# Loading one activation block behind the V weights instead of ahead of them, at the start of a fused attention and gated-MLP kernel

## The chip, the cores and the metric

The kernel runs on one core of one Trainium2 chip. The metric is the device time of one execution in microseconds (us). A ratio given with an interval is computed as the mean time of one kernel's runs over that of the other kernel's runs of the same rounds, so it is not quite the ratio of the medians that are quoted beside it. A profile is one execution taken by the hardware profiler; its times count from the start of the span. A transfer's landing is the last of the 16 increments of its semaphore (a counter that others wait on) in the trace; these (5.84 to 6.47 us for the V weights of the kernel before) are taken as one from each of the 16 DMA engines that the page names. The granted clock is the share of PE's full clock that the trace records for a stretch.

Engines: PE is TensorE (matmuls), PEld its weight loads (for a transpose of a block they load `xn`, for a V matmul the transposed block `xnT`; the V weights are the other operand), DVE is VectorE, ACT is ScalarE, POOL is GpSimd, SP is the sync engine, which issues 54 of the 56 DMAs in the trace of the kernel before.

## The reference, cut to what matters

```python
x = A_x                                  # 1 x 2048 x 512, bf16
xn = _layernorm(x, axis=-1)              # (x - mean) / sqrt(var + 1e-5), row by row
return x + _A_ref(xn, A_wqkv, A_wo) + _B_ref(xn, B_w_gate, B_w_up, B_w_down)
# _A_ref: 32 heads of 16, causal attention in a window of 256; qkv = xn @ wqkv, then @ wo
# _B_ref: ((xn @ w_gate) * (xn @ w_up)) @ w_down, inner size 1792
```

## The kernel before

The 2048 rows are 16 blocks of 128 rows, four blocks to a chunk. Before PE can do useful work, the blocks of the first chunk must be loaded, normalised, transposed and multiplied with the V weights. These are the loads (`self.x[:, t, :]` is block t; the first 512 columns of `Wqkv` are Q, then K, then V):

```python
for lo, hi in ((0, 1), (1, 2), (2, 4)):
    nc.sync.dma_start(out=self.x[:, lo:hi, :], in_=xv[:, lo:hi, :])
for lo in (1024, 512, 0):                      # V, K, Q weights, 512 KB each
    nc.sync.dma_start(out=self.Wqkv[:, :, lo:lo + 512], in_=wq[:, :, lo:lo + 512])
# ... gate, up, x blocks 4 to 7, gate, up, down, Wo: cut ...
for lo, hi in ((8, 10), (10, 12), (12, NT)):
    nc.sync.dma_start(out=self.x[:, lo:hi, :], in_=xv[:, lo:hi, :])
```

And this is the order of work on the first chunk. `norm_stats` is two DVE instructions (statistics `st`, then mean and variance `mv`), `norm_scale` computes the inverse deviation `rs` on POOL (for block 0 partly on DVE), `norm_apply` makes the normalised block `xn` on DVE, `norm_transpose` is four PE transposes with a copy by ACT, `proj_v` four V matmuls with a copy to `V`.

```python
def first_chunk(self):
    self.new_chunk(0)
    for b in range(2):
        self.norm_stats(b, 1)
        self.norm_scale(b, 1)
    for b in (0, 1, 2):
        self.norm_apply(b)
        if b < 2:
            self.norm_stats(b + 2, 1)
            self.norm_scale(b + 2, 1)
    self.norm_transpose(0, False)
    self.keep_busy(8)                          # spare matmuls
    for b in range(4):
        if b < 3:
            self.norm_transpose(b + 1, False)
        self.proj_v(b, engine="act" if b == 2 else "dve")
        if b == 0:
            self.norm_apply(3)
    # ... K and Q projections, copies of V by DMA from ACT's queue: cut ...
```

The softmax here doesn't subtract the row's maximum and nothing guards it: scores larger than these inputs give would overflow.

## Time and profile before

| what | value | where from |
|---|---|---|
| time | 263.29 us, median of 3 (263.16 to 263.78) | timed runs |
| profiled span | 261.2 us, PE busy 98% | head and first part of the page |
| first V matmul | 6.67 us | timeline of PE |
| first K matmul | 10.76 us | timeline of PE |
| V weights landed | 6.47 us | semaphore increments in the trace |

A span with PE busy for 98% is read as one long line of matmuls: whatever delays PE by a microsecond at the start should be there at the end too, unless PE later waits for something that does not move with it. The lines behind this are shown in the prediction.

### The profile page before, as it was taken

How to read it: one execution, taken by the hardware profiler on the slowest of the kernel's cores; microseconds unless marked ns; L12 is line 12 of the kernel's file. 1: busy time of each engine (PE TensorE's matmuls, PEld its weight loads, DVE VectorE, ACT ScalarE, POOL GpSimd, SP SyncE). 2: the span in 40 equal slices, each digit the busy share in tenths (PEclk: the TensorE clock that was granted, in tenths of full speed). 3: DMA queues.
4: the chain of work that ended last, by engine and by line, in shares of the span. 5: the costliest groups of instructions: out<-in, count | busy, mean ns of one | idle time of the engine just before them, and what ended most of it. 6: DMA issues, size and time to landing. Idle time of an engine off the chain costs nothing.

```text
span 261.2 us, 7718 instructions
## 1 busy us (share of the span) xinstructions
PE 255.8 (98%) x3154; PEld 118.0 (45%) x3170; DVE 179.5 (69%) x357; ACT 176.4 (68%) x143; POOL 116.0 (44%) x278
## 2 busy tenths in 40 slices
PE   8999999999999999999999999999999999999995
PEld 8444444444344544444544454344544445444453
DVE  6787888779846597557974769767795235977344
ACT  3477688888757776678775567767787546787600
POOL 6225342425457644333457644544443451464600
PEclk9999999999999999999999999999999999999999
DMA  6999910120012300002001310001000100000002
GB/s 193 379 350 341 286 30 20 24 48 1 3 37 46 83 3 1 3 0 48 3 3 40 84 43 3 0 1 29 23 3 0 42 24 20 5 0 3 1 3 83
DMA packets 19427, 15.05 MB, mean 58 GB/s; under 512 B 7360, under 2 KB 19392, under 8 KB 19392
## 3 DMA queue, kind: packets, MB, share of 16 engines
q1 hardware_dynamic: 18848, 14.26, 18.6%
q8 instruction: 26, 0.43, 0.7%
q10 hardware_dynamic: 544, 0.30, 0.4%
q14 instruction: 9, 0.07, 0.1%
HBM read 9.70 MB, written 2.10 MB: 45 GB/s over the span
## 4 chain that ended last, share of the span: by engine, by line
PE 98%; issue 1%; DVE 0%
PE gp L399 19%; PE up L410 19%; PE psd L432 17%; PE qkp L255 11%; PE S L317 10%; PE acc L370 7%; PE vp L243 5%; PE psd L438 5%; PE L L432 2%; PE wps L131 2%; PE L L438 1%; PE xTp L213 0%; PE L L370 0%; DVE x L448 0%; DVE idle L95 0%
## 5 line engine op out<-in xcount | busy, mean ns | idle before, releaser
L323 ACT ACTIVATE P<-S 128x2048 bf16<-128x2048 f32 x75 | 140.7, 1876 | 49.6 <-PE S L317 41.0
L162 POOL TENSOR_SCALAR_AFFINE_SELECT P<-P 64x256 bf16<-64x256 bf16 x224 | 99.7, 445 | 123.7 <-ACT P L323 108.6
L399 PE MATMUL gp<-xnT,Wg 128*128 128x512 bf16 x224 | 60.1, 380 | 0.0
L410 PE MATMUL up<-xnT,Wu 128*128 128x512 bf16 x224 | 59.1, 380 | 0.0
L415 DVE TENSOR_TENSOR hT<-up,gsb 128x512 bf16<-128x512 f32 x56 | 38.3, 684 | 18.3 <-PE up L410 13.1
L432 PE MATMUL psd<-Wd,hT 128*128 128x512 bf16 (+1 forms) x202 | 46.9, 369 | 0.8 <-issue 0.6
L347 DVE TENSOR_TENSOR P<-P,diag 128x512 bf16<-128x512 bf16 (+1 forms) x75 | 29.6, 394 | 5.9 <-ACT P L323 5.9
L432 PEld LDWEIGHTS <-hT 128*128 128x128 bf16 x238 | 21.3, 98 | 25.3 <-issue 3.5
L410 PEld LDWEIGHTS <-Wu 128*128 128x128 bf16 x224 | 20.4, 98 | 25.6 <-issue 3.3
L399 PEld LDWEIGHTS <-Wg 128*128 128x128 bf16 x224 | 20.3, 98 | 25.3 <-issue 3.3
L317 PE MATMUL S<-Q,K 32*128 32x320 bf16 (+4 forms) x720 | 29.8, 254 | 0.1
L255 PE MATMUL qkp<-xnT,Wqkv 128*128 128x512 bf16 x128 | 29.9, 380 | 0.0
L234 ACT ACTIVATE gsb<-gp 128x512 bf16<-128x512 f32 x38 | 22.3, 596 | 7.7 <-PE gp L399 6.9
L317 PEld LDWEIGHTS <-K 32*128 32x128 bf16 x720 | 10.3, 92 | 30.7 <-issue 30.3
L376 DVE STREAM_TRANSPOSE at<-acc 128x512 f32<-128x512 f32 x30 | 19.1, 688 | 6.5 <-PE acc L370 6.4
L448 DVE TENSOR_TENSOR x<-psd,x 128x512 bf16<-128x512 f32 (+1 forms) x15 | 9.7, 655 | 15.7 <-PE psd L438 15.7
L255 PEld LDWEIGHTS <-Wqkv 128*128 128x128 bf16 x128 | 11.7, 98 | 14.7 <-issue 1.8
L370 PE MATMUL acc<-P,VS 64*32 64x320 bf16 (+4 forms) x672 | 17.7, 253 | 0.0
L370 PE MATMUL acc<-P,V 64*32 64x320 bf16 (+4 forms) x672 | 17.5, 253 | 0.0
L370 PEld LDWEIGHTS <-V 64*32 64x32 bf16 x720 | 15.1, 91 | 2.3 <-issue 1.7
L243 PE MATMUL vp<-Wqkv,xnT 128*128 128x512 bf16 x60 | 14.9, 380 | 0.3 <-issue 0.2
L370 PEld LDWEIGHTS <-VS 64*32 64x32 bf16 x720 | 14.7, 91 | 0.6 <-issue 0.2
(54 smaller groups left out, 180.5 us busy)
## 6 DMA issues: line engine op xcount, KB each, us to landing
out_dram<-x SPq DMA_DIRECT2D x15, 128.0 KB, 1.8
Wg<-in_B_w_gate_dram SPq DMA_DIRECT2D x2, 896.0 KB, 11.2
Wu<-in_B_w_up_dram SPq DMA_DIRECT2D x2, 896.0 KB, 12.6
Wd<-in_B_w_down_dram SPq DMA_DIRECT2D x1, 1792.0 KB, 17.4
Wqkv<-in_A_wqkv_dram SPq DMA_DIRECT2D x3, 512.0 KB, 6.3
x<-in_A_x_dram SPq DMA_DIRECT2D x2, 512.0 KB, 8.6
VS<-V SPq DMA_DIRECT2D x6, 144.0 KB, 2.6
x<-in_A_x_dram SPq DMA_DIRECT2D x3, 256.0 KB, 4.8
```

The costliest lines, as they stand in the source:

```text
L162: nc.gpsimd.affine_select(out=v, in_=v, pattern=pattern + [[1 if diag else -1, 64]], compare_op=ALU.is_ge if diag else ALU.is_gt, fill=0.0 ...
L234: nc.scalar.activation(out=out, in_=in_, func=ACT.Copy)
L243: nc.tensor.matmul(ps[:], lhsT=self.xnT[T][:, b, k, :], rhs=self.Wqkv[:, k, 1024:1536], start=(k == 0), stop=(k == 3))
L255: nc.tensor.matmul(ps[:], lhsT=self.Wqkv[:, k, lo:lo + 128], rhs=self.xnT[T][:, :, k, :], start=(k == 0), stop=(k == 3))
L317: nc.tensor.matmul(S[:, e, col:col + n], lhsT=self.K[U, c][rows, keys], rhs=self.Q[T, c][rows, q:q + n], start=True, stop=True, tile_posit ...
L323: nc.scalar.activation(out=P[:, :, 0:col], in_=S[:, :, 0:col], func=ACT.Exp, scale=0.25)
L347: self.nc.vector.tensor_tensor(out=v, in0=v, op=ALU.min, in1=self.diag.unsqueeze(1).unsqueeze(1).to_broadcast([128, 4, n, 64]))
L370: nc.tensor.matmul(accs[par][32 * e:32 * e + 32, q:q + n], lhsT=v, rhs=P[rows, e, col:col + n], start=(i == 0), stop=(i == len(todo) - 1), ...
L399: nc.tensor.matmul(ps[:], lhsT=self.Wg[:, k, 128 * f:128 * f + 128], rhs=self.xnT[T][:, :, k, :], start=(k == 0), stop=(k == 3))
L410: nc.tensor.matmul(ps[:], lhsT=self.Wu[:, k, 128 * f:128 * f + 128], rhs=self.xnT[T][:, :, k, :], start=(k == 0), stop=(k == 3))
L415: nc.vector.tensor_tensor(out=self.hT[T, f][:], in0=ps[:], in1=self.gsb[:], op=ALU.mult)
L432: nc.tensor.matmul(ps, lhsT=self.hT[T, f][:, 128 * b:128 * b + 128], rhs=self.Wd[:, f, c0:c1], start=(f == 0), stop=False)
```

## The change

Its intent: block 2 comes alone, the V weights have 128 KB less in front of them, and block 3, wanted last, comes behind them. To keep the number of loads, blocks 8 to 11 are merged.

```diff
-        for lo, hi in ((0, 1), (1, 2), (2, 4)):
+        for lo, hi in ((0, 1), (1, 2), (2, 3)):
             nc.sync.dma_start(out=self.x[:, lo:hi, :], in_=xv[:, lo:hi, :])
         for lo in (1024, 512, 0):
             nc.sync.dma_start(out=self.Wqkv[:, :, lo:lo + 512], in_=wq[:, :, lo:lo + 512])
+            if lo == 1024:
+                nc.sync.dma_start(out=self.x[:, 3:4, :], in_=xv[:, 3:4, :])
...
-        for lo, hi in ((8, 10), (10, 12), (12, NT)):
+        for lo, hi in ((8, 12), (12, NT)):
             nc.sync.dma_start(out=self.x[:, lo:hi, :], in_=xv[:, lo:hi, :])
```

## The prediction

> **What bounds the kernel now.** I read the page's first and fourth parts first, to see which engine sets the time.
>
> ```profile
> span 261.2 us, 7718 instructions
> PE 255.8 (98%) x3154; PEld 118.0 (45%) x3170; DVE 179.5 (69%) x357; ACT 176.4 (68%) x143; POOL 116.0 (44%) x278
> ...
> PE 98%; issue 1%; DVE 0%
> ```
>
> The span is one long TensorE (PE) program: 255.8 of 261.2 us are matmul time, and the chain that ended last is PE for 98%. [...] the change can matter only where it moves a PE wait. The diff touches loads of the first few microseconds, so I then read the timeline of VectorE (DVE) from 2.9 to 9.1 us, where the four blocks of x are normalised: `st` is the statistics of a block, `mv` their mean and variance, `xn` the normalised block. The columns are start, busy time, engine, line, operation, tiles, and in brackets the idle time before it and what ended that.
>
> ```profile
> 2.97 0.70 DVE L173 BATCH_NORM_STATS2 st<-x 128x6 f32<-128x512 bf16 x1 [0.95 <-DMA x<-in_A_x_dram]
> ...
> 3.99 0.68 DVE L173 BATCH_NORM_STATS2 st<-x 128x6 f32<-128x512 bf16 x1
> ...
> 5.10 0.68 DVE L173 BATCH_NORM_STATS2 st<-x 128x6 f32<-128x512 bf16 x1
> 5.82 0.18 DVE L174 BATCH_NORM_AGGREGATE mv<-st 128x2 f32<-128x6 f32 x1
> 5.96 0.41 DVE L194 TENSOR_SCALAR xn<-x,mv,rs 128x512 bf16<-128x512 bf16 x1
> 6.29 0.69 DVE L173 BATCH_NORM_STATS2 st<-x 128x6 f32<-128x512 bf16 x1
> 7.01 0.18 DVE L174 BATCH_NORM_AGGREGATE mv<-st 128x2 f32<-128x6 f32 x1
> 7.14 0.41 DVE L194 TENSOR_SCALAR xn<-x,mv,rs 128x512 bf16<-128x512 bf16 x1
> 7.73 0.69 DVE L236 CAST V<-vp 128x512 bf16<-128x512 f32 x1 [0.18 <-PE vp L243]
> 8.34 0.40 DVE L194 TENSOR_SCALAR xn<-x,mv,rs 128x512 bf16<-128x512 bf16 x1
> ```
>
> Only block 0's statistics wait for a transfer. From 2.97 to 7.55 DVE runs without a gap, so it is DVE's own pace, not the loads of blocks 1 to 3, that spaces the normalised blocks. Note the program order: the statistics of block 3 (6.29) stand in front of the `xn` of block 2 (7.14). Next, the weight-load side of PE in the same stretch, to see which of these DVE results PE waits for:
>
> ```profile
> 6.43 0.23 PEld L213 LDWEIGHTS <-xn 128*128 128x128 bf16 x4
> 6.62 0.58 PEld L243 LDWEIGHTS <-xnT 128*128 128x128 bf16 x4
> 7.60 0.23 PEld L213 LDWEIGHTS <-xn 128*128 128x128 bf16 x4 [0.40 <-DVE xn L194]
> 7.79 0.58 PEld L243 LDWEIGHTS <-xnT 128*128 128x128 bf16 x4
> 8.80 0.23 PEld L213 LDWEIGHTS <-xn 128*128 128x128 bf16 x4 [0.43 <-DVE xn L194]
> ```
>
> PE transposes block 2 at 7.60 and block 3 at 8.80, both times released by DVE's `xn`. The matmul records show how much of these waits is real: the last V matmul of block 0 starts at 7.32 and holds PE for 0.22 us, so PE is free at 7.53 and starts again at 7.61; for block 3 it is free at 8.71 and starts at 8.80. So PE already waits some 0.08 and 0.1 us there: it has no slack against DVE. The first V matmul, at 6.67, follows the transposes of block 1 at the same 0.056 us step that these have among themselves; it does not wait for its weights.
>
> **Landings.** From the trace's record of semaphore increments by the DMA, counted from the start of the span: block 0 at 2.94, block 1 at 3.40, blocks 2 and 3 at 4.63, V weights at 6.47, K weights at 8.56, Q weights at 10.05 us. After 4.63 three loads of 512 KB take 5.42 us, so 128 KB take 0.45 us.
>
> [...] they land in the order of issue. [...] DVE's order is the program's, and no PE matmul passes the transposes waiting at 7.60. [...]
>
> **The change, part by part.** The listings of both kernels' instruction streams are the same on PE, DVE, ACT and POOL but for which DMA semaphore a few of them wait on.
>
> (1) Block 2 alone, 128 KB instead of 256. It lands some 0.45 us earlier, near 4.2 instead of 4.63. Its statistics start at 5.10 because DVE is busy before: gain 0.
>
> (2) V weights with 128 KB less in front: they land near 6.47 - 0.45 = 6.02. PE wants them at 6.62 and is held until then by the `xn` of block 1 (ends 6.37) and the transposes after it. Gain 0 in the profiled run; what improves is only the margin, from about 0.1 to 0.6 us.
>
> (3) Block 3 behind the V weights. In front of the end of its load there are now as many bytes as were in front of the end of the V load (1024 KB), so it lands at about 6.47, and with some 0.03 us from landing to start (as for block 0: 2.94 and 2.97) its statistics start at 6.50 instead of 6.29: 0.21 us later. [...] mean and variance go from 7.01 to 7.22, the `xn` of block 2 from 7.14 to 7.35, its end from 7.55 to 7.76. PE, free at 7.53, waits 0.21 us more for the transposes of block 2. Block 3's own chain: its POOL steps hang on its mean and variance and move by the same 0.21, so `xn` of block 3 goes from 8.34 to 8.55, when PE, itself 0.21 later, wants it. From there on the V matmuls of blocks 2 and 3, the K and Q projections and all that follows move as one, since K and Q weights (8.56, 10.05) land well before their matmuls (10.76, 11.63). I find no wait further down that is tied to a fixed time: gate and up weights are wanted at 18.5 and 19.4 and land at 12.5 and 14.9. So the 0.21 us stays to the end.
>
> (4) One load more in front of the gate weights, one less at the end. The transfers rotate over eight semaphores, so waits shift by one. The first up-weight load must now wait for block 0 (landed 2.94, issue after 4.3): 0. The merged load of blocks 8 to 11 saves one issue of about 0.4 us on the sync queue. Blocks 12 to 15 no longer wait for the down weights (28.82) and go out at about 25 us; the first transpose for the next chunk now waits for the down weights instead, at the same time as before (issue 29.3). Its result is wanted by PE at 49.4: 0.
>
> Sum: 0 + 0 + 0.21 + 0 = +0.21 us on 263.29, which gives 263.5.
>
> **The rivals.** (A) A gain: outside the profiler the V weights come later than 6.62 in most runs, so PE waits for them before, and the change takes that away. For it: the margin of 0.1 us is small. Against it: the V load lands later only together with everything on the queue, so block 3 comes later too, and its wait replaces the other. At best about -0.3 us, 263.0. (B) The last of the 16 engines is slow for block 3, which then lands 0.3 to 0.5 us after the estimate: the increments for the V weights are spread over 0.64 us, those for the K weights over 1.17. Then PE loses 0.5 to 0.7 us, 263.9. (C) Block 3 lands before 6.29, as the fast engines pass on to it while the slow one ends the V weights: no change, 263.3. Its own slowest engine decides, so I hold this for less likely than the main case. (D) Something in the middle, say the transposes of the next chunk queued behind the earlier load of blocks 12 to 15: PE would have to wait at 49.4, about 15 us after the first of them lands now (34.4); the last one is issued at 48 on an empty queue either way. I give it next to nothing.
>
> **Range and chances.** The branches A to C span 263.0 to 263.9; the three runs of before lie between 263.16 and 263.78, so run to run spread is as large as the effect. I take 262.9 to 264.2 as the range. Two per cent would be 5.3 us, more than the whole stretch from the first V matmul to the first Q matmul; no step comes near it: 0.01 faster, 0.98 within 2%, 0.01 slower.
>
> **What would show it right or wrong.** Right: in the changed kernel's DVE timeline the fourth statistics (block 3) shows a wait for the load of x that ends at about 6.5; the `xn` of block 2 starts at about 7.35; PE's transposes of block 2 start at about 7.8 and the first K matmul at about 10.97 instead of 10.76, while the first V matmul stays at 6.67. Step 3 is wrong if no such wait appears, or if the lag of 0.2 us is gone by the first exponential (14.15 before). Step 2 is wrong if the first V matmul moves earlier. The whole is wrong if the span differs by over 1 us.

Cut from this record are rules on the order in which engines and queues work that were not taken from this case's traces, and my premise that the bytes in front of a load decide when it lands. No term of the sum goes with them: it came to 0 + 0 + 0.21 + 0 = +0.21 us, 263.5. The landings of 6.02 in step (2) and 6.47 in step (3) are estimates, worked out from the V weights' landing at 6.47 and from 0.45 us per 128 KB (5.42 us for three loads of 512 KB).

## The result

The changed kernel takes 264.06 us (median of 6, 263.88 to 264.36) against 263.28 us (median of 6) for the kernel before: ratio 1.0028, 95% interval 1.0015 to 1.0040. It is a little slower, clear of noise, and inside the forecast range. The forecast was 263.5, so of the 0.78 us between the medians it foresaw 0.21, about a quarter.

The head, first and fourth parts of the page of the changed kernel:

```profile
span 262.1 us, 7734 instructions
PE 257.0 (98%) x3170; PEld 117.1 (45%) x3170; DVE 179.6 (69%) x357; ACT 176.4 (67%) x143; POOL 115.6 (44%) x278
...
PE 96%; DVE 2%; DMA 1%; issue 0%
```

The chain that ended last now leaves PE: 2% of it is DVE and 1% a DMA. (PE's busy time is not to be compared to a tenth: before, 16 matmul records are missing from the trace, 3154 instead of 3170.) The timeline of DVE in the same stretch as before:

```profile
5.02 0.69 DVE L175 BATCH_NORM_STATS2 st<-x 128x6 f32<-128x512 bf16 x1
...
5.88 0.41 DVE L196 TENSOR_SCALAR xn<-x,mv,rs 128x512 bf16<-128x512 bf16 x1
6.90 0.69 DVE L175 BATCH_NORM_STATS2 st<-x 128x6 f32<-128x512 bf16 x1 [0.60 <-DMA x<-in_A_x_dram]
7.62 0.18 DVE L176 BATCH_NORM_AGGREGATE mv<-st 128x2 f32<-128x6 f32 x1
7.72 0.40 DVE L196 TENSOR_SCALAR xn<-x,mv,rs 128x512 bf16<-128x512 bf16 x1
8.04 0.69 DVE L238 CAST V<-vp 128x512 bf16<-128x512 f32 x1
8.89 0.41 DVE L196 TENSOR_SCALAR xn<-x,mv,rs 128x512 bf16<-128x512 bf16 x1 [0.16 <-POOL rs L188]
```

The fourth statistics, those of block 3, wait 0.60 us for the load of x and start at 6.90 instead of 6.29. The next `xn`, that of block 2, starts at 7.72 instead of 7.14, though block 2 itself was there in good time (landed at 3.94). The weight-load side of PE:

```profile
6.35 0.23 PEld L215 LDWEIGHTS <-xn 128*128 128x128 bf16 x4 [0.51 <-DVE xn L196]
6.62 0.56 PEld L245 LDWEIGHTS <-xnT 128*128 128x128 bf16 x4
8.18 0.23 PEld L215 LDWEIGHTS <-xn 128*128 128x128 bf16 x4 [1.00 <-DVE xn L196]
...
9.36 0.23 PEld L215 LDWEIGHTS <-xn 128*128 128x128 bf16 x4 [0.41 <-DVE xn L196]
```

The first V matmuls stand where they stood, at 6.62, but by coincidence: before, the transposes of block 1 held them (6.43 to 6.62); here these start at 6.35, and the first V weight load starts 0.105 us after the V weights landed (6.516). The transposes of block 2 come at 8.18 instead of 7.60, those of block 3 at 9.36 instead of 8.80. I then laid the two lists of PE's 3170 weight loads beside each other: from the transposes of block 2 (+0.577) to the very last one (+0.565, at 258.83 instead of 258.27) the distance stays between 0.557 and 0.577 us. The whole loss on PE is made at one place and kept to the end.

The profiled span grew by 0.9 us, so some 0.3 us lie behind PE's end: from the start of the last DVE addition to the end of the span it is 2.60 us before and 2.93 after. In the twelve further profiles this tail is between 2.59 and 2.92 us, 2.91 in one whose PE ended as in the kernel before, so I take it for scatter of the last stores.

### The profile page after: what moved, and what is told of

The parts are those of the page before. It is cut to its first block, busy times and chain, and to the rows that moved or that the text cites. A ratio compares the mean times of both kernels' runs of the same rounds, so it can differ in the third digit from the quotient of the medians.

```text
span 262.1 us, 7734 instructions
## 1 busy us (share of the span) xinstructions
PE 257.0 (98%) x3170; PEld 117.1 (45%) x3170; DVE 179.6 (69%) x357; ACT 176.4 (67%) x143; POOL 115.6 (44%) x278
## 4 chain that ended last, share of the span: by engine, by line
PE 96%; DVE 2%; DMA 1%; issue 0%
PE gp L401 19%; PE up L412 19%; PE psd L434 17%; PE qkp L257 11%; PE S L319 9%; PE acc L372 7%; PE vp L245 5%; PE psd L440 5%; PE L L434 2%; DMA x<-in_A_x_dram 1%; DVE st L175 1%; PE L L440 1%; PE L L372 0%; PE xTp L215 0%; DVE xn L196 0%; DVE mv L176 0%
## 5 line engine op out<-in xcount | busy, mean ns | idle before, releaser
L434 PE MATMUL psd<-Wd,hT 128*128 128x512 bf16 (+1 forms) x210 | 48.0, 369 | 0.0
## 6 DMA issues: line engine op xcount, KB each, us to landing
Wu<-in_B_w_up_dram SPq DMA_DIRECT2D x2, 896.0 KB, 12.4
```

The costliest lines, as they stand in the source:

```text
L434: nc.tensor.matmul(ps, lhsT=self.hT[T, f][:, 128 * b:128 * b + 128], rhs=self.Wd[:, f, c0:c1], start=(f == 0), stop=False)
```

## The experiments

Theory 1: the only cost is the wait of block 3's statistics; DVE's order hands it to block 2, and PE keeps it. Theory 2: the merged load and the shifted semaphore waits cost too. Theory 3: the new order of the queue costs by itself, because the weights come later. Every kernel was also profiled, and "PE's end" below is the shift of its last weight load against the profile of the kernel before.

### Each part of the change alone

The changed kernel with blocks 8 to 11 in two loads again:

```diff
-        for lo, hi in ((8, 12), (12, NT)):
+        for lo, hi in ((8, 10), (10, 12), (12, NT)):
```

> Only the move of block 3; blocks 8 to 11 stay in two loads. Theory 1 (the statistics of block 3 wait for its late load, and DVE's order hands that wait to PE): +0.6 to +0.8 us on the kernel before, statistics of block 3 starting near 6.9 us, as in the changed kernel. Theory 2 (the merged load of blocks 8 to 11, and the semaphore waits that it shifts, cost part of the 0.8 us): about +0.5 us, less than the changed kernel by 0.2 or more.

The kernel before with only the merge:

```diff
-        for lo, hi in ((8, 10), (10, 12), (12, NT)):
+        for lo, hi in ((8, 12), (12, NT)):
```

> Only the merge of blocks 8 to 11; blocks 2 and 3 together as before. Theory 1: within 0.15 us of the kernel before, start-up unchanged (transposes of block 2 near 7.6 us). Theory 2: slower by 0.2 us or more.

Measured: move alone 264.00 us (ratio 1.0015, 0.9992 to 1.0039), merge alone 263.61 (0.9997, 0.9977 to 1.0018), against 263.55 for the kernel before in these rounds, which had two outliers (264.06 and 265.09) and so wide intervals. By its median the merge alone (+0.06) is where theory 1 has it, but the move alone (+0.45) is nearer to theory 2's +0.5 than to theory 1's +0.6 to +0.8, and the intervals settle neither. The profiles say more. With the merge alone block 3's statistics start at 6.13 without a wait. PE's end is 0.22 us late all the same, but all of it is made before the first V matmul (6.84 instead of 6.62): the transposes of block 1 follow each other at up to 0.11 us instead of 0.06. The trace's first record of the full clock is at 6.74 us here and at 6.27 in the kernel before. That moment varies from 3.86 to 6.74 over the 14 profiles (4.33 and 6.42 in the two of the changed kernel), so I put the 0.22 down to the run and not to the merge. With the move alone block 3's statistics start at 7.58: in this one profile V weights and block 3 landed at 7.17 and 7.55, later than in any other with this order, and PE's end is 1.26 us late. So the V weights' landing varied by over half a microsecond from run to run (6.34 to 7.17 with this order).

### The wait taken away, the queue kept

The changed kernel, but block 3's statistics are taken of block 2's data. The result is wrong (relative error 0.05).

```diff
-        nc.vector.bn_stats(out=st[:], in_=self.x[:, t, :])
+        nc.vector.bn_stats(out=st[:], in_=self.x[:, 2 if t == 3 else t, :])
```

> The changed kernel, but the statistics of block 3 are taken of block 2's data (result wrong on purpose), so that nothing but the normalised block 3 needs block 3's load, at about 8.3 us. Theory 1: the wait at the fourth statistics is gone, the transposes of block 2 are back near 7.6 us and the time is back at that of the kernel before, within 0.15 us, though every load is queued as in the changed kernel. Theory 3 (the queue order itself costs, for the weights land later): it stays +0.5 us or more.

Measured: 263.63 us against 263.55, ratio 1.0003 (0.9983 to 1.0023). DVE's timeline of this kernel has its old pace, with all loads queued as in the changed kernel:

```profile
6.30 0.69 DVE L175 BATCH_NORM_STATS2 st<-x 128x6 f32<-128x512 bf16 x1
7.03 0.18 DVE L176 BATCH_NORM_AGGREGATE mv<-st 128x2 f32<-128x6 f32 x1
7.16 0.41 DVE L196 TENSOR_SCALAR xn<-x,mv,rs 128x512 bf16<-128x512 bf16 x1
```

But in this profile PE's end was still 0.68 us late, for another reason. ACT's timeline shows it; the first two lines are from this kernel:

```profile
12.79 2.38 ACTq L155 DMA_DIRECT2D VS<-V  x2
15.21 1.88 ACT L325 ACTIVATE P<-S 128x2048 bf16<-128x2048 f32 x1 [1.91 <-DVE K L267]
```

and these are the same two of the kernel before:

```profile
12.77 1.32 ACTq L153 DMA_DIRECT2D VS<-V  x2
14.15 1.88 ACT L323 ACTIVATE P<-S 128x2048 bf16<-128x2048 f32 x1 [0.86 <-PE S L317]
```

ACT needed 2.38 instead of 1.32 us to issue its two copies of V, so its first exponential came 1.07 us late. I ran the same kernel again:

> The same kernel as stats_other_data, because its first profile showed a second, later delay: the copies of V issued by ACT took 2.38 instead of 1.32 us at 12.8 us and held up the first exponential by 1.07 us and PE by 0.67. If that is a chance meeting on the queues, this profile shows 1.3 us there and PE's end within 0.15 us of the kernel before; if it belongs to this order of loads, it is there again. Times: within 0.2 us of the kernel before either way by the first run's median.

Measured: 263.31 us against 263.42, ratio 0.9997 (0.9985 to 1.0010). The two issues took 1.34 us this time, and PE's end is at +0.08. The long issue was not seen in any other of the 14 profiles, so I take it for chance. Theory 3 falls as the cause of the loss: with the changed queue but without the wait it is gone (the interval leaves at most +0.26 us).

### The wait put in, the queue untouched

The kernel before, with a spare statistics instruction in front of block 3's:

```diff
         st = self.small.tile([128, 6], F32, tag="st")
+        if t == 3:
+            spare = self.const.tile([128, 6], F32, name="spare")
+            nc.vector.bn_stats(out=spare[:], in_=self.x[:, 0, :])
         nc.vector.bn_stats(out=st[:], in_=self.x[:, t, :])
```

> The kernel before, all loads as before, with one spare statistics instruction (of block 0, result unused) in front of the statistics of block 3: DVE is held up by about 0.66 us at the same place, and no load is touched. Theory 1: +0.6 us, +0.5 to +0.75, like the changed kernel: the delay on DVE is all of it. Theory 3: less than +0.3 us, for DVE would catch up and the loss be the queue's.

Measured: 263.80 us against 263.55 (1.0010, 0.9990 to 1.0030), too wide to tell +0.6 from nothing, because of the outliers named above; so once more:

> The same kernel as dve_delay, because the kernel before had two slow outliers in that round and the interval was wide. Theory 1: +0.4 to +0.6 us in the times, PE's last weight load 0.53 us late as in the first profile.

Measured: 263.81 us against 263.36, ratio 1.0019 (1.0007 to 1.0032). DVE's timeline of the first of the two:

```profile
6.26 0.69 DVE L175 BATCH_NORM_STATS2 spare<-x 128x6 f32<-128x512 bf16 x1
6.87 0.68 DVE L176 BATCH_NORM_STATS2 st<-x 128x6 f32<-128x512 bf16 x1
7.58 0.18 DVE L177 BATCH_NORM_AGGREGATE mv<-st 128x2 f32<-128x6 f32 x1
7.68 0.41 DVE L197 TENSOR_SCALAR xn<-x,mv,rs 128x512 bf16<-128x512 bf16 x1
```

The times of the statistics and of `xn` are the changed kernel's within 0.04 us, without touching a load, and PE's end is 0.54 and 0.53 us late in the two profiles (0.57 in the changed kernel). So a delay of about 0.6 us at this place on DVE is enough for the whole loss on PE. One more set of rounds of the changed kernel, for comparison in size:

> The changed kernel once more, for a second profile and more times. +0.5 to +0.9 us on the kernel before. On the landing of the V weights: if the bytes in front decide, 6.0 us in most profiles and the 6.52 of the first was chance; if V weights start slowly whatever stands in front, again 6.4 us or later, and block 3 about 0.35 us after it.

Measured: 263.84 us against 263.42, ratio 1.0018 (1.0005 to 1.0030), PE's end +0.50. The median, +0.42, is just under the +0.5 to +0.9 expected. With the first rounds (+0.78, ratio 1.0028) the loss is 0.4 to 0.8 us; a part of 0.2 beyond PE's shift is not settled by these numbers. Compared in size, the delay by DVE work alone (+0.45 in `dve_delay_2`) costs as much as the whole change here (+0.42), which leaves no visible part for theory 2.

### The order on DVE turned

If DVE's order hands block 3's wait to block 2, one could turn it. This is the changed kernel with block 2's `xn` first:

```diff
-        for b in (0, 1, 2):
-            self.norm_apply(b)
-            if b < 2:
-                self.norm_stats(b + 2, 1)
-                self.norm_scale(b + 2, 1)
+        self.norm_apply(0)
+        self.norm_stats(2, 1)
+        self.norm_scale(2, 1)
+        self.norm_apply(1)
+        self.norm_apply(2)
+        self.norm_stats(3, 1)
+        self.norm_scale(3, 1)
```

> The changed kernel with DVE's order turned: the normalisation of block 2 in front of the statistics of block 3, so that the wait for block 3's load can't reach block 2. If the order on DVE is the whole cause: block 2's transposes back at 7.6 us and a time below the changed kernel's. If block 3's own chain (statistics, mean and variance, two POOL steps, normalisation) is as tight: block 2 back at 7.6, but block 3's transposes at about 9.8 us (8.80 before, 9.36 in the changed kernel), and the kernel +1.0 us on the kernel before, slower than the changed kernel by 0.4.

Measured: 264.27 us against 263.36, ratio 1.0033 (1.0020 to 1.0046), PE's end +0.99. The weight-load side of PE:

```profile
7.56 0.23 PEld L215 LDWEIGHTS <-xn 128*128 128x128 bf16 x4 [0.32 <-DVE xn L196]
...
9.79 0.23 PEld L215 LDWEIGHTS <-xn 128*128 128x128 bf16 x4 [1.46 <-DVE xn L196]
```

Block 2's transposes are back at 7.56, but block 3's are now at 9.79 instead of 9.36: its statistics start at 7.42, behind the `xn` of block 2, which waits until 7.09 for a POOL step, and two POOL steps follow them. The cure moves the wait from block 2 to block 3 and makes it longer. This shows that DVE's order is how the wait reaches block 2. It does not show what the late load costs in this order: block 3 had landed at 6.81, so here the order, not the load, sets 7.42.

### Block 3 later still, and the clock

One load further back, behind the K weights:

```diff
-            if lo == 1024:
+            if lo == 512:
                 nc.sync.dma_start(out=self.x[:, 3:4, :], in_=xv[:, 3:4, :])
```

> Block 3 one load further back, behind the K weights. Theory 1 (each microsecond of delay of block 3 reaches the end): its load lands near 8.5 us, the fourth statistics start there instead of 6.29, +2.2 us on the kernel before (+1.9 to +2.5), all of it already in the transposes of block 2. Rival (later stages have slack that absorbs part): under +1.5 us.

Measured: 266.93 us (265.67 to 267.41) against 263.42, ratio 1.0126 (1.0103 to 1.0149). The wait is as expected, block 2's transposes are 2.09 us late, but the time lost is over 3 us. From 11.2 us on PE's V matmuls follow each other at 0.43 instead of 0.22 us (the granted clock is 0.50 from 10.7 to 14.1 us), and the first K matmul's weights are 3.66 us late. To see whether PE's clock fell while it waited, I filled the wait with spare matmuls (in `first_chunk`, at the head of the loop over b):

```diff
         for b in range(4):
+            if b == 1:
+                self.keep_busy(32)
             if b < 3:
```

> behind_k with 32 spare matmuls on PE in front of the transposes of block 2, which fill 1.8 us of PE's wait. There the wait was 2.1 us and the kernel 3.5 us slower; the granted clock was 0.73 from 9.6 to 12 us. If the extra 1.5 us come from the clock that fell while PE idled: clock 1.0 throughout and +2.1 us (+1.9 to +2.4) on the kernel before. If they come from something else (late weights): +3.5 us as before.

The view of busy times by stretches, for 9.6 to 12 us; the columns are busy us and instructions of PE, PEld, DVE, ACT and POOL, then the granted clock, the DMA share and GB/s. First without the filler, then with it:

```profile
9.60:12.00 2.40, 2.30 (x14) 1.27 (x15) 1.74 (x4) 1.04 (x2) 0.68 (x2) 0.73 1.06 381
```

```profile
9.60:12.00 2.40, 2.29 (x17) 1.10 (x18) 1.76 (x4) 1.19 (x2) 0.70 (x2) 1.00 1.07 388
```

The granted clock in this stretch is 0.73 without (full at first, then half) and 1.00 with the filler, and with it the first K matmul is 2.08 us late: the wait and nothing on top. The unfilled kernel's own runs agree: three with a mean clock of 0.994 took 266.89 to 267.41, the one with 1.000 took 265.67, which is 2.25 above the kernel before. Theory 1 holds for the wait, one to one, and in three of the four unfilled runs the wait of 2 us was followed by a lower clock as well. The filler kernel's total, 270.78 us (ratio 1.0285), missed the expectation badly: PE loses another 4.9 us later on, most of it at 91 us (2.0) and 188 us (2.1). The filler takes one more tile of the program's four-deep PSUM pool than the kernel before; what makes the later waits no run here shows, and I use only its start.

### When the V weights land

The prediction wanted the V weights at 6.02; they came at 6.52. Two kernels vary what is in front of them. V weights behind blocks 0 and 1 only, from the changed kernel:

```diff
-        for lo, hi in ((0, 1), (1, 2), (2, 3)):
+        for lo, hi in ((0, 1), (1, 2)):
...
-                nc.sync.dma_start(out=self.x[:, 3:4, :], in_=xv[:, 3:4, :])
+                nc.sync.dma_start(out=self.x[:, 2:4, :], in_=xv[:, 2:4, :])
```

> V weights with only 256 KB in front (blocks 0 and 1), blocks 2 and 3 together behind them. Landing of the V weights: 5.6 us if the bytes in front decide; 5.9 us or later if the V load has a slow start of its own, 6.4 or later if it does not depend on what stands in front. Time: the third statistics wait for blocks 2 and 3 until 6.2 to 6.9 us instead of 5.10, and the normalisation of block 1 stands behind them, so theory 1 has the transposes of block 1 1.1 to 1.8 us late and the kernel as much slower.

And all four blocks ahead, each with its own load, from the kernel before (with the merge of blocks 8 to 11):

```diff
-        for lo, hi in ((0, 1), (1, 2), (2, 4)):
+        for lo, hi in ((0, 1), (1, 2), (2, 3), (3, 4)):
```

> Blocks 0 to 3 in four loads of 128 KB, all ahead of the V weights, and blocks 8 to 11 merged: the changed kernel's number of loads and its rotation of semaphores, but not its order. Theory 1 (only the place of block 3 behind the V weights costs): within 0.2 us of the kernel before, block 3's statistics at 6.3 us without a wait. Rival (one more load ahead, or the shifted waits, cost): +0.4 us or more.

Measured: V after one 265.44 us against 263.42, ratio 1.0061 (1.0045 to 1.0076); block 2's statistics wait until 7.24, and block 1's transposes are 2.07 us late, more than the 1.1 to 1.8 expected. In the profiled run the clock fell again (0.50 from 9.1 to 12.4 us; mean 0.994, 267.10 us); the other four have mean clocks of 0.998 to 1.000 and took 264.76 to 265.57. Four loads: 263.86 against 263.36, ratio 1.0015 (1.0001 to 1.0028), which is not what theory 1 expected. Its DVE does keep the old pace (block 3's statistics at 6.23, no wait), but PE's weight loads show this:

```profile
6.36 0.23 PEld L213 LDWEIGHTS <-xn 128*128 128x128 bf16 x4 [0.51 <-DVE xn L194]
7.28 0.56 PEld L243 LDWEIGHTS <-xnT 128*128 128x128 bf16 x4 [0.69 <-issue]
```

The first V matmul waits until 7.28, for the V weights, which landed at 7.17, with the same 512 KB in front as in the kernel before, where they landed at 6.47. What differs is that SP issues them fifth, not fourth, 0.48 us later. PE's end is 0.64 us late. That suggested to set the landing against the time of issue. This table is worked out from the increments that the 16 DMA engines give the load's semaphore (us; "mean" over the 16, "last" the one that counts):

```
kernel                KB in front  issued  mean   last   mean - issued
v_after_one               256       1.71   5.59   6.46      3.88
after                     384       2.17   6.17   6.52      4.00
after_2                   384       2.16   5.90   6.45      3.74
move_alone                384       2.17   6.10   7.17      3.93
stats_other_data          384       2.17   6.21   6.47      4.04
stats_other_data_2        384       2.17   6.07   6.34      3.90
apply_first               384       2.17   6.13   6.44      3.96
behind_k                  384       2.16   6.08   6.52      3.92
behind_k_busy             384       2.16   5.97   6.53      3.81
before                    512       2.17   6.21   6.47      4.04
merge_alone               512       2.17   6.15   6.60      3.98
dve_delay                 512       2.17   6.12   6.57      3.95
dve_delay_2               512       2.17   6.32   6.53      4.15
four_loads                512       2.65   6.62   7.17      3.97
```

The V weights land, in the mean of the engines, 3.7 to 4.2 us after their issue, whether 256, 384 or 512 KB stand in front. At the same issue time, 128 KB less in front bring 0.12 us (mean of the eight 6.08, of the four 6.20), not 0.45. The same can be seen in the view by stretches, from 3.5 to 4.5 us; first the kernel before, then the changed one:

```profile
3.50:4.50 1.00, 1.00 (x12) 1.00 (x11) 0.93 (x4) 0.00 (x0) 0.35 (x1) 1.00 1.02 277
```

```profile
3.50:4.50 1.00, 1.00 (x13) 1.00 (x12) 0.93 (x4) 0.00 (x0) 0.42 (x1) 1.00 0.77 120
```

Before, the DMA engines move 277 GB/s here, the second half of blocks 2 and 3; after, with block 2 done at 3.94, only 120. The room that the shorter queue makes is not filled: 122 packets start instead of 286, and they take 102 ns each in the mean instead of 57. Why a load of 512 KB does not flow sooner after its issue these runs do not show. Nor do they part the time of issue from the place in SP's order: no run delays the issue alone. Block 3 lands 0.36 to 0.39 us behind the V weights in all six profiles with that order (6.87 in the changed kernel).

No version beat the kernel before. In its profile the transposes hold the first V matmul, so an earlier load has little to give. But the margin is thin: in seven of the 14 profiles, the changed kernel's first among them, the first V weight load starts 0.105 us after the V weights' landing and later than the transposes alone would have let it. Taking 0.105 us as the step from landing to start, the margin in the kernel before is an estimated 0.04 us (6.62 against 6.47 + 0.105).

## Why the prediction was right, and where its size was off

- **The total: inside the range, but thanks to its width.** The range was drawn for the rivals and the spread of the runs (262.9 to 264.2); the sum of the steps, +0.21, is well below the 0.4 to 0.8 measured. The signs named for the main case came in kind, each some 0.4 us later than named: the wait at the fourth statistics ends at 6.90 (6.5), `xn` of block 2 starts at 7.72 (7.35), block 2's transposes at 8.18 (7.8), the first K matmul at 11.32 (10.97).
- **What bounds the kernel: right.** PE keeps a delay made at 8 us until 258 us, to 0.02 us.
- **Step (1), block 2 alone, gain 0: right.** It landed at 3.94 instead of 4.63 (4.2 forecast), and its statistics start when DVE is free (5.02).
- **Step (2), the V weights land near 6.02: wrong in its premise, right in its gain of 0.** They landed at 6.52. The premise, an estimate of mine, was that the bytes in front decide when a load lands; here the landing went with the issue (3.7 to 4.2 us after it, in the mean of the engines), which the change leaves at 2.17. So the margin did not grow by 0.5 us as forecast: in the changed kernel's first profile it was gone, and the first V matmul stayed in its place partly by luck.
- **Step (3), block 3 lands at 6.47 and costs 0.21: right in mechanism, off in size.** Every link was found: the wait at the fourth statistics, the `xn` of block 2 behind it, PE's transposes, nothing absorbed later. The mis-sized term is the landing of block 3, taken from step (2): 6.87 instead of 6.47. That made the statistics 0.61 late and PE 0.57. Taking the wait away brought the time back (0.9997), and a delay put in by DVE work alone gave PE 0.53 to 0.54.
- **Step (4), semaphore rotation and the merged load, 0: not contradicted.** The traces of both kernels have DMA increments on eight semaphores, as it said. Merge alone gave 0.9997, in a wide interval, and PE's distance to the kernel before stays within 0.02 us from 8 us to the end, so nothing is lost on PE further down.
- **Rival A** (V weights already late before) was not the outcome: the kernel did not gain. That the margin is small was right, even more so than it said (0.04 us, see above). What a late landing does is seen in `four_loads`: 7.17, and the first V weight load at 7.28.
- **Rival B** named the size that came, 0.5 to 0.7 us, but for another reason: not one slow engine, the mean of the 16 was late as well (6.54).
- **Rivals C and D** did not come: block 3 landed at 6.81 to 6.87 in the changed kernel's two profiles, not before 6.29, and PE gains no wait near 49 us. What rival C supposed is seen in part: block 3's first increment came at 6.06, before the V weights' last at 6.52, but its own last came at 6.87.

## What to carry to other kernels

A load that is moved back should still land before its engine reaches the instruction that wants it, for that instruction may stand in front of work for other data. Here DVE kept the program's order: block 3's statistics waited 0.60 us, and block 2's `xn` behind them started at 7.72 instead of 7.14; in `v_after_one` block 2's statistics waited 2.10 us, and block 1's `xn` behind them started at 8.07 instead of 5.96. In the first microseconds of a kernel, set a load's landing against its issue time before counting the bytes in front of it: here the one load more ahead of the V weights put off their issue by 0.48 us and their landing by 0.4 (mean of the engines), and 128 KB taken away gave back 0.12. A wait of 0.6 us on PE cost 0.6 us here; one of 2 us was followed by a lower clock in four of nine runs of `behind_k` and `v_after_one` (mean 0.994; in their profiles 0.50 from 10.7 to 14.1 and from 9.1 to 12.4 us).
